# Output products of a fused attention and SwiGLU kernel: 48 plain products a block against seven half products of 2x2 blocks

## The chip, the cores and the metric

The kernel runs on one core of a Trainium2 chip. The metric is the device time of one execution in microseconds. Its engines run side by side, each with a queue of its own, and meet at semaphores: TensorE (PE in the profile, its weight loads PEld), VectorE (DVE), ScalarE (ACT), GpSimd (POOL) and SyncE (SP), which issues DMAs.

## The reference

A linear attention with cosine weights, then an RMS norm and a SwiGLU feed-forward layer. Batch 8, 8 heads, 576 positions, head dimension 64, so 4608 tokens of 512 features; the inner dimension is 1536.

```python
r = maximum(x, 0); phi = concatenate([r * cos_w, r * sin_w], axis=-1)      # for q and k
kv = einsum('bhsf,bhsd->bhfd', k_p, v); z = sum(k_p, axis=2)
attn = einsum('bhsf,bhfd->bhsd', q_p, kv) / (einsum('bhsf,bhf->bhs', q_p, z) + 1e-6)
x = attn as (B * S, H * D)
xn = x / sqrt(mean(x * x) + 1e-6) * rms_g
h = silu(xn @ w_gate) * (xn @ w_val)                                       # 4608 x 1536
out = h @ w_out                                                            # 4608 x 512
```

## The kernel before, in words

The tokens are worked in nine blocks of 512. Blocks 0 to 7 hold 512 positions of one batch each; block 8 holds the tails, the last 64 positions of all eight batches. Before the change the order is 0, 1, 2, 3, 4, 5, 6, 8, 7.

A block has two parts. First come 12 gate and value steps (`gval_step`): step n multiplies the 512 normed tokens with 128 columns of `w_gate` (four matmuls of 512 columns into a psG bank, `half_mm`, L556) and of `w_val` (four into a psV bank). ScalarE takes the silu of the gate (L570), VectorE multiplies it with the value into tile n of `hT` (L571). Then come four output steps (`out_step`): each gives 128 tokens their 512 outputs with 12 matmuls of 512 columns, weights from `hT`, moving operand `wo` (`out_mm`, L574), in psC banks. ScalarE copies the bank to SBUF (L286) and SyncE stores it (L585; 64 rows at a time for blocks 0 and 8, L592). Of block 7, worked last, the last 128 tokens are split by columns into 256, 160 and 96.

The attention of batch b+1 is worked inside block b. The order of all this is written out by hand: `at(blk, n, where, f, ...)` registers a call for a slot of step n of block blk, and `run` makes the calls at that place. "pe" is before the step's matmuls, "mid" between gate and value, "pre" before the silu and the multiply, "post" after them; steps 12 to 15 are the output steps. The order in a slot is the order of registration, and each engine, and SyncE's queue of DMAs, keeps the order in which the calls come.

For one batch the calls are these. The loads of k, v and q for batch nb go to a ring of five `raw` buffers, from SyncE, in steps 0, 3 and 6 of block nb-2 (steps 3, 5, 8 of block 2 and 4, 8, 12 of block 1). `k_phi` makes phi of k (L292 on ScalarE, L294 on VectorE) and `v_cast` rounds v to bf16 (L288), both in the output steps of block nb-2. `q_phi` makes phi of four groups of 128 queries, each followed by a transpose through a DMA of SyncE (`q_tr_dma`, L346): in steps 14, 15, 0 and 1 (for batch 3 one step later). `kvz_pe` makes the key-value products in step 2 (L387, L394). `nd_pe` makes the attention outputs of group j (L449) in steps 4, 6, 8 and 10; `nd_post` divides them on VectorE (L489, L492, L499), `x_sq` sums squares on ScalarE (L515) and takes the power -1/2 on GpSimd (L520), and one step later `x_norm` scales them on VectorE (L527) and `x_tr_dma` transposes them through a DMA (L540) for the next block. The tails of two batches at a time go the same way (`load_q_tails`, `q_tails_phi`, `nd_tails_pe`, L474), spread over blocks 2, 3, 4 and 6.

The program has eight semaphores for DMAs of SyncE, used in turn; a DMA waits for the one issued eight before it.

Of the kernel before, what the change touches and what calls it, by code (L numbers as in the profile page):

```python
# [9 lines left out]
FP32 = mybir.dt.float32  # L10
# [7 lines left out]
def kernel(  # L18
# [15 lines left out]
    P = 128  # L34
# [16 lines left out]
    ring = ctx.enter_context(tc.tile_pool(name="ring", bufs=5))  # L51
    two = ctx.enter_context(tc.tile_pool(name="two", bufs=2))
    four = ctx.enter_context(tc.tile_pool(name="four", bufs=4))
    six = ctx.enter_context(tc.tile_pool(name="six", bufs=6))
# [84 lines left out]
    def load_q_tails(pair):  # L139
        rqt[pair] = two.tile([P, H, D], FP32, name="rqt", tag="rqt")  # L140
# [69 lines left out]
    vv0 = one.tile([P, HP, NC * D], BF16, name="vv0")  # L210
# [61 lines left out]
    vv = one.tile([P, HP, NC, E], BF16, name="vv")  # L272
# [5 lines left out]
    xnT_tail = one.tile([P, NDT, TB], BF16, name="xnT_tail")  # L278
# [73 lines left out]
    def q_tails_tr_dma(pair):  # L352
        t = qp_of(("t", pair))
        qpTt[pair] = one.tile([P, H, P], BF16, name="qpTt", tag="qpTt")
# [82 lines left out]
    def kvz0_evac(eng, g):  # L437
        if 0 not in kvzs:
            kvzs[0] = six.tile([P, 2, HP * E], BF16, name="kvzs", tag="kvzs")
        copy(eng, kvzs[0][:, g, :], psG[g][:, 0 : HP * E])  # L440

    def kvz_evac(eng, b):
        kvzs[b] = six.tile([P, 2, HP * E], BF16, name="kvzs", tag="kvzs")
# [123 lines left out]
    def gval_h(blk, n):  # L567
        g, v = banks_of(blk, n)
        sg = four.tile([P, TB], FP32, name="sg", tag="sg")
# [9 lines left out]
    def out_store(eng, blk, j, bank, cols=(0, DM)):  # L579
        osb = four.tile([P, DM], FP32, name="osb", tag="osb")  # L580
        w = cols[1] - cols[0]
        copy(eng, osb[:, 0:w], bank[:, 0:w])
        if 0 < blk < 8:
            rows = out[blk * S : blk * S + 512, :].rearrange("(p j) m -> p j m", j=4)
            nc.sync.dma_start(out=rows[:, j, cols[0] : cols[1]], in_=osb[:, 0:w])  # L585
            return
        for i in range(2):
            b, c = (0, 2 * j + i) if blk == 0 else (2 * j + i, NC - 1)
            rows = out[b * S + 512 : b * S + S, :]
            if b == 0:  # L590
                rows = out[0:S, :].rearrange("(s c) m -> s c m", c=NC)[:, c, :]
            nc.sync.dma_start(  # L592
                out=rows[:, cols[0] : cols[1]], in_=osb[64 * i : 64 * i + 64, 0:w]
# [70 lines left out]
    def unit_silu(i):  # L664
        sg_of[i] = four.tile([P, TB], FP32, name="sg", tag="sg")
# [95 lines left out]
    KCS5 = ((0, 1), (2,), (3,), (4,))  # L761
# [34 lines left out]
    def last_step():  # L796
# [5 lines left out]
        sg = four.tile([P, TB], FP32, name="sg", tag="sg")  # L802
# [18 lines left out]
    for nb in range(2, B):  # L821
        b = nb - 1
        first = nb == 2
        for i, cs in enumerate(KCS5 if wide(nb) else KCS):
            kb, kn = ((0, 14), (0, 15), (1, 0), (1, 1))[i] if first else (b - 1, 12 + i)
            for c in cs:
                at(kb, kn, "post", k_phi, V, nb, c, 0)
                at(kb, kn, "post", k_phi, A, nb, c, 1)
        for i in range(2):
# [8 lines left out]
        kz = 3 if first else 2  # L838
        at(b, kz, "pe", kvz_pe, nb)
        at(b, kz, "pre", kvz_evac, A, nb)  # L840
        for j in range(4):
            n = ((6, 8, 9, 11) if first else (4, 6, 8, 10))[j]
            at(b, n, "mid" if n == 9 else "pe", nd_pe, nb, j)
            at(b, n, "pre", nd_post, nb, j)
            at(b, n, "post", x_sq, nb, j)
            m = n + 2 if first and j == 0 else n + 1
# [3 lines left out]
    for pair in range(4):  # L850
        b = 2 * pair or 3
        at(*((2, 13), (1, 13), (3, 9), (5, 9))[pair], "post", load_q_tails, pair)
        at(b, 3, "post", q_tails_phi, V, pair, 0)
        at(b, 3, "post", q_tails_phi, A, pair, 1)
        at(b, 3, "post", q_tails_tr_dma, pair)
# [103 lines left out]
```

## Time and profile before

| what | value |
|---|---|
| three runs | 322.76, 323.32 and 323.61 us; median 323.32 |
| profiled execution, span from first to last instruction | 321.1 us |
| what lies around the span, against the median | 2.2 us |
| mean granted TensorE clock | 1.000 |
| blocks 3 and 4 (121.29 to 155.06 and 155.06 to 188.80) | 33.77 and 33.74 us, of which PE is busy 33.56 and 33.53, VectorE 21.57, ScalarE 19.07 |
| HBM read and written | 37.83 and 9.44 MB, 147 GB/s over the span |

The durations below are of that one execution. Busy time of an engine is the time in which it runs instructions; matmuls are pipelined, so the time of many in a row says more than the duration of one (0.38 us each, but 0.86 for four of 512 columns). The chain that ended last is followed back from the last instruction, at each step to what released it. A DMA's landing is the time from its issue to the semaphore that tells of its end; not every DMA has one in the trace.

### The profile page before, as it was taken

To read this page: it belongs to the slowest core of one execution; us is meant where nothing else is said; L and a number is where in the kernel's file an instruction comes from. 1 tells how busy PE (TensorE), PEld (TensorE's weight loads), DVE (VectorE), ACT (ScalarE), POOL (GpSimd) and SP (SyncE) were. 2 spreads that over 40 slices of the span, in tenths; PEclk is the share of its full clock that TensorE was granted. 3 is DMA by queue.
4 is the path that set the end of the run, shared out by engine and by line. 5 is a ranking of instruction groups with operands and counts; after the bars stand their busy time and mean duration, and the time that the engine had idled before them with its cause. 6 is when DMAs were issued, how large, how long until landed. Compare 5 with 4: busy or idle time off the path is not lost.

```text
span 321.1 us, 6023 instructions
## 1 busy us (share of the span) xinstructions
PE 313.6 (98%) x2274; PEld 162.4 (51%) x2310; DVE 185.4 (58%) x382; ACT 165.8 (52%) x322; POOL 40.5 (13%) x79
## 2 busy tenths in 40 slices
PE   7999999999999999999999999999999999999996
PEld 2689564544454445444544445544544444444444
DVE  7976977668457773777457644781676034204410
ACT  5766756754574466554744575446543233223321
POOL 9771211002001100010001100100011000000000
PEclk9999999999999999999999999999999999999999
DMA  7999999788999999999799959995522500041002
GB/s 232 239 270 269 282 329 227 201 183 190 223 226 211 187 263 187 221 247 182 162 186 230 197 163 200 197 217 163 99 59 41 116 33 0 0 102 31 1 35 98
DMA packets 80092, 53.76 MB, mean 167 GB/s; under 512 B 52235, under 2 KB 74047, under 8 KB 80063
## 3 DMA queue, kind: packets, MB, share of 16 engines
q1 hardware_dynamic: 73110, 41.25, 62.1%
q0 software_dynamic: 6944, 12.13, 15.5%
q8 instruction: 18, 0.29, 0.4%
q14 instruction: 12, 0.09, 0.1%
q10 hardware_dynamic: 8, 0.00, 0.0%
HBM read 37.83 MB, written 9.44 MB: 147 GB/s over the span
## 4 chain that ended last, share of the span: by engine, by line
PE 94%; DMA 2%; DVE 1%; issue 1%; POOL 1%; ACT 0%; POOLq 0%; ACTq 0%
PE psC L574 27%; PE psV L556 27%; PE psG L556 26%; PE psV L643 2%; PE psA L449 2%; DMA vv<-in_v_dram 2%; PE psG L574 2%; PE psG L643 2%; PE psA L387 2%; PE psA L394 1%; PE psA L474 0%; PE psV L363 0%; PE psG L430 0%; PE psC L546 0%; POOL raw L135 0%
## 5 line engine op out<-in xcount | busy, mean ns | idle before, releaser
L571 DVE TENSOR_TENSOR hT<-psV,sg 128x512 bf16<-128x512 f32 x99 | 68.2, 689 | 96.5 <-PE psV L556 64.1
L556 PE MATMUL psV<-xnT,wv 128*128 128x512 bf16 x344 | 89.6, 379 | 0.7 <-issue 0.2
L570 ACT ACTIVATE sg<-psG 128x512 f32<-128x512 f32 x99 | 58.6, 592 | 60.8 <-PE psG L556 52.7
L556 PE MATMUL psG<-xnT,wg 128*128 128x512 bf16 x337 | 88.5, 379 | 0.7 <-issue 0.2
L574 PE MATMUL psC<-wo,hT 128*128 128x512 bf16 (+1 forms) x400 | 88.4, 376 | 0.4
L574 PEld LDWEIGHTS <-hT 128*128 128x128 bf16 x456 | 43.1, 98 | 47.7
L556 PEld LDWEIGHTS <-wv 128*128 128x128 bf16 x400 | 39.0, 98 | 46.8
L556 PEld LDWEIGHTS <-wg 128*128 128x128 bf16 x400 | 37.0, 98 | 39.9 <-DVE xnT L288 0.2
L520 POOL TENSOR_TENSOR rs<-ms,mhalf 128x1 f32<-128x1 f32 x36 | 20.5, 570 | 193.9 <-ACT scr L515 193.7
L286 ACT COPY osb<-psC 128x512 f32<-128x512 f32 x32 | 18.7, 585 | 49.9 <-PE psC L574 46.1
L515 ACT ACTIVATE scr<-xt 128x513 bf16<-128x513 f32 x36 | 22.8, 635 | 23.3 <-DVE xt L499 22.3
L527 DVE SCALAR_TENSOR_TENSOR xn<-xt,rs,gb 128x512 bf16<-128x512 f32 (+1 forms) x37 | 26.9, 730 | 9.9 <-POOL rs L520 9.9
L292 ACT ACTIVATE kp<-raw,tab 128x256 bf16<-128x256 f32 (+2 forms) x51 | 28.8, 607 | 2.4 <-DMA raw<-in_k_dram 2.4
L499 DVE TENSOR_TENSOR xt<-psA,rec 128x512 f32<-128x512 f32 x36 | 24.9, 691 | 1.2
L292 ACT ACTIVATE qp<-raw,tab 128x512 bf16<-128x512 f32 (+1 forms) x36 | 23.3, 666 | 1.2 <-DMA raw<-in_q_dram 1.1
L294 DVE TENSOR_SCALAR kp<-raw,tab 128x256 bf16<-128x256 f32 (+2 forms) x53 | 20.1, 428 | 0.5 <-DMA raw<-in_k_dram 0.5
L294 DVE TENSOR_SCALAR qp<-raw,tab 128x512 bf16<-128x512 f32 (+1 forms) x34 | 15.3, 463 | 4.7 <-DMA raw<-in_q_dram 4.7
L449 PEld LDWEIGHTS <-qpT 128*128 128x128 bf16 x224 | 10.6, 97 | 6.6
L556 PE MATMUL psV<-xnT_tail,wv 128*128 128x512 bf16 x48 | 12.3, 379 | 0.1
L556 PE MATMUL psG<-xnT_tail,wg 128*128 128x512 bf16 x46 | 12.0, 379 | 0.1
L288 DVE CAST vv<-raw 116x1280 bf16<-116x1280 f32 (+1 forms) x13 | 11.1, 857 | 1.3 <-DMA raw<-in_v_dram 1.3
L449 PE MATMUL psA<-kvzs,qpT 128*128 128x65 bf16 x224 | 11.4, 193 | 0.0
(102 smaller groups left out, 177.7 us busy)
## 6 DMA issues: line engine op xcount, KB each, us to landing
out_dram<-osb SPq DMA_DIRECT2D x27, 256.0 KB, 2.3
raw<-in_q_dram SPq DMA_DIRECT2D x6, 1024.0 KB, 9.1
raw<-in_k_dram SPq DMA_DIRECT2D x5, 1120.0 KB, 8.8
raw<-in_v_dram SPq DMA_DIRECT2D x5, 1120.0 KB, 9.4
raw<-in_k_dram POOLq DMA_DIRECT2D x2, 1152.0 KB, 19.2
raw<-in_v_dram POOLq DMA_DIRECT2D x2, 1152.0 KB, 15.7
out_dram<-osb SPq DMA_DIRECT2D x17, 128.0 KB, 2.6
wg<-in_moe_w_gate_dram POOLq DMA_DIRECT2D x3, 512.0 KB, 13.8
```

The source lines that it names most:

```text
L286: A.copy(out=o, in_=i)
L292: A.activation(out=out_ap, in_=in_ap, func=AF.Relu, scale=scale)
L294: eng.tensor_scalar(out=out_ap, in0=in_ap, scalar1=scale, scalar2=0.0, op0=ALU.mult, op1=ALU.max)
L449: nc.tensor.matmul(heads[:, g, hp, :], lhsT=qpT[:, h, j * P : (j + 1) * P], rhs=kvzs[b][:, g, hp * E : (hp + 1) * E], start=True, stop=True,)
L499: V.tensor_tensor(out=xt[:, 0:DM].rearrange("p (hp g d) -> p g hp d", g=2, d=D), in0=heads[:, :, :, 0:D], in1=rec[:, :, :].unsqueeze(3).to ...
L515: A.activation(out=scr[:, :], in_=xt[:, 0 : DM + 1], func=AF.Square, scale=1.0 / math.sqrt(DM), accum_out=ms[:, :],)
L520: G.tensor_tensor(out=rs[:, :], in0=ms[:, :], in1=mhalf[:, :], op=ALU.pow)
L527: V.scalar_tensor_tensor(out=xn_of[(b, j)][:, c], in0=x_of[(b, j)][:, c], scalar=rs_of[(b, j)][:, :], in1=gb[:, c], op0=ALU.mult, op1=ALU. ...
L556: nc.tensor.matmul(bank[:, cols[0] : cols[1]], lhsT=w[:, t, n * P : (n + 1) * P], rhs=x[:, t, cols[0] : cols[1]], start=(t == 0), stop=(t ...
L570: A.activation(out=sg[:, :], in_=g[:, 0:TB], func=AF.Silu)
L571: V.tensor_tensor(out=hT[:, n, :], in0=v[:, 0:TB], in1=sg[:, :], op=ALU.mult)
L574: nc.tensor.matmul(bank[:, 0 : cols[1] - cols[0]], lhsT=hT[:, n, j * P : (j + 1) * P], rhs=wo[:, n, cols[0] : cols[1]], start=(n == 0), st ...
```

## The change

The output part of blocks 1 to 8 is made as a product of 2x2 blocks with seven products in place of eight (Strassen's form). Tokens are halved (256 and 256), the inner dimension is halved (`NM` = 6 tiles of 128 each) and the output columns are halved (`HC` = 256). Each of the seven products is made for two groups p of 128 tokens, with 6 matmuls of 256 columns: 84 matmuls a block. The sums of the inputs are tiles of their own: five sums of `wo` (`wsum`, made once, three on GpSimd and two on VectorE) and per block the sums of `hT` halves on VectorE (`s12` in two parts, `s0`, `s3`, `s4`). The sums of the outputs are made in PSUM: products are added onto a bank that ScalarE has copied out in between, or that VectorE or ScalarE has written, and VectorE subtracts at the end (`q_end`).

The rest follows from the room and the time that this takes. `raw` has four buffers, `sg` three, `osb` two of twice the width, `kvzs` eight; `vv`, `vv0` share room with the sums and `xnT_tail`, `qpTt` with `kp5`; the tails' queries are loaded into `raw`. Block 8 is worked last, and all tails are worked in block 7. From batch 3 on, `v_cast` is on GpSimd, `k_phi` is mostly on ScalarE and in slots "act" inside the output part, and `q_phi` with its transposes is in steps 0, 1, 2 and 4, with the attention outputs in steps 3, 5, 7 and 9. The slots of the loads are the same. The core of the diff:

```diff
+    def h_sum12(m0, m1):
+        V.tensor_tensor(
+            out=s12[:, m0:m1, :], in0=hT[:, m0:m1, :], in1=hT[:, NM + m0 : NM + m1, :],
+            op=ALU.add,
+        )
...
+    def prod(i, p, dst, first=False, cols=(0, HC)):
+        c0, c1 = p * P, p * P + HC
+        lhs = {
+            1: (s0, 0, c0), 2: (s12, 0, c1), 3: (hT, 0, c0), 4: (hT, NM, c1),
+            5: (s12, 0, c0), 6: (s3, 0, c0), 7: (s4, 0, c0),
+        }[i]
...
+            nc.tensor.matmul(
+                dst, lhsT=t[:, o + m, c : c + P], rhs=w,
+                start=(first and m == 0), stop=(m == NM - 1), skip_group_check=True,
+            )
...
-            vb, vn = ((0, 15), (1, 0))[i] if first else (b - 1, 13 + 2 * i)
-            at(vb, vn, "post", v_cast, V, nb, (2 * i, 2 * i + 2))
+            for i in range(3):
+                at(b - 1, 12 + 2 * i, "act", k_phi, A, nb, i, 0)
+                at(b - 1, 13 + 2 * i, "act", k_phi, A, nb, i, 1)
+            for i in range(2):
+                at(b - 1, 12, "dve", k_phi, V, nb, 3, i)
+                at(b, 0, "post", k_phi, (V, A)[i], nb, 4, i)
+                vb = (1, 14 + i) if nb == 3 else (b - 1, 8 + 2 * i)
+                at(*vb, "post", v_cast, G, nb, (2 * i, 2 * i + 2))
         for j in range(4):
-            late = j + (nb == 3)
-            qb, qn = (b, 1 + j) if first else (b - (late < 2), (14 + late) % 16)
-            at(qb, qn, "post", q_phi, V, nb, j, 0)
-            at(qb, qn, "post", q_phi, A, nb, j, 1)
-            at(qb, qn, "post", q_tr_dma, nb, j)
+            n = 1 + j if nb == 2 else (0, 1, 2, 4)[j]
+            at(b, n, "post", q_phi, V, nb, j, 0)
+            at(b, n, "post", q_phi, A, nb, j, 1)
+            at(b, n, "post", q_tr_dma, nb, j)
...
-            n = ((6, 8, 9, 11) if first else (4, 6, 8, 10))[j]
+            n = ((6, 8, 9, 11) if nb == 2 else (3, 5, 7, 9))[j]
...
+        at(*((6, 1), (6, 4), (7, 2), (7, 4))[pair], "post", load_q_tails, pair)
+        b, n = 7, 2 * pair + 1
+        at(b, n, "post", q_tails_phi, V, pair, 0)
+        at(b, n, "post", q_tails_phi, A, pair, 1)
+        at(b, n, "post", q_tails_tr_dma, pair)
+        at(b, n + 3, "pe", nd_tails_pe, pair)
...
+        at(b, n + 4, "post", x_norm, 2 * pair + 1, 4)
+        at(b, n + 4, "post", x_tr_dma, 2 * pair + 1, 4)
...
+        if blk and n == NNT - 1:
+            h_sum12(0, NM // 2)
         gval_h(blk, n)
...
+    def out_step(blk):
...
+        def begin(p):
+            bank = bq[p][0]
+            prod(3, p, bank[:, 0:HC], first=True)
+            prod(4, p, bank[:, HC:DM])
+            osb[p] = osb_tile()
+            run(blk, 12 + p, "act")
+            A.copy(out=osb[p][:, mid], in_=bank[:, :])
...
+        h_sum12(NM // 2, NM)
+        begin(0)
+        run(blk, 12, "post")
+        begin(1)
+        q_start(0)
+        h_sum0()
+        run(blk, 13, "post")
+        prod(5, 0, bq[0][0][:, 0:HC])
+        prod(2, 0, bq[0][0][:, HC:DM])
+        run(blk, 14, "act")
+        side(0)
+        q_start(1)
+        h_sum4()
+        prod(5, 1, bq[1][0][:, 0:HC])
+        prod(1, 0, bq[0][1][:, 0:HC])
+        run(blk, 15, "act")
+        A.copy(out=bq[0][1][:, HC:DM], in_=bq[0][1][:, 0:HC])
+        h_sum3()
+        run(blk, 14, "post")
+        prod(2, 1, bq[1][0][:, HC:DM])
+        prod(1, 1, bq[1][1][:, 0:HC])
+        run(blk, 16, "act")
+        side(1)
...
+        run(blk, 12, "dve")
...
+        prod(7, 0, bq[0][1][:, 0:HC])
+        prod(6, 0, bq[0][1][:, HC:DM])
+        q_end(0)
+        prod(7, 1, bq[1][1][:, 0:HC])
+        if blk < last_blk:
+            prod(6, 1, bq[1][1][:, HC:DM])
+            q_end(1)
...
-    for blk in (1, 2, 3, 4, 5, 6, 8, 7):
+    for blk in range(1, 9):
```

`side` copies the two outer sums of a group out of PSUM, `q_start` writes the first two products' sum into the other bank, and in block 8 `side` and `q_end` issue a store for each half of 64 rows and 256 columns: 18 stores in all for that block.

More of the change, by code (lines that the diff above doesn't have):

```diff
@@ L139, in load_q_tails @@
     def load_q_tails(pair):
-        rqt[pair] = two.tile([P, H, D], FP32, name="rqt", tag="rqt")
+        t = ring.tile([P, H * NC5 * D], FP32, name="raw", tag="raw")
+        rqt[pair] = t[:, 0 : H * D].rearrange("p (h d) -> p h d", h=H)
         for i in range(2):
@@ L577, in out_mm, with osb_tile, store @@
         )
[L579 to L582, printed above, removed]
+    def osb_tile():
+        return two.tile([P, 2 * DM], FP32, name="osb", tag="osb")
+    def store(blk, j, cols, src):
         if 0 < blk < 8:
             rows = out[blk * S : blk * S + 512, :].rearrange("(p j) m -> p j m", j=4)
-            nc.sync.dma_start(out=rows[:, j, cols[0] : cols[1]], in_=osb[:, 0:w])
+            nc.sync.dma_start(out=rows[:, j, cols[0] : cols[1]], in_=src)
             return
@@ L591, in out_store @@
                 rows = out[0:S, :].rearrange("(s c) m -> s c m", c=NC)[:, c, :]
-            nc.sync.dma_start(
-                out=rows[:, cols[0] : cols[1]], in_=osb[64 * i : 64 * i + 64, 0:w]
+            nc.sync.dma_start(out=rows[:, cols[0] : cols[1]], in_=src[64 * i : 64 * i + 64])
+    def out_store(eng, blk, j, bank, osb):
+        copy(eng, osb, bank[:, 0:DM])
+        store(blk, j, (0, DM), osb)
+    s12 = hsum[:, 0 : NM * TB].rearrange("p (m s) -> p m s", m=NM)
+    s0, s3, s4 = [
+        hsum[:, NM * (TB + i * HC) : NM * (TB + (i + 1) * HC)].rearrange(
+            "p (m s) -> p m s", m=NM
+        )
+        for i in range(3)
+    ]
@@ L760 @@
     KCS = ((0, 1, 2), (3, 4), (5, 6), (7, 8))
-    KCS5 = ((0, 1), (2,), (3,), (4,))
     for c in range(NC):
@@ L801, in last_step @@
         kvz_pe(1)
-        sg = four.tile([P, TB], FP32, name="sg", tag="sg")
+        sg = three.tile([P, TB], FP32, name="sg", tag="sg")
         A.activation(out=sg[:, :], in_=g[:, 0:TB], func=AF.Silu)
```

177 lines of the change are left out of this document (126 added, 51 removed).

## The prediction

> **What bounds the kernel now.** I read the busy times first, then the chain that ended last, then the chain in order of time, and then the queue of SyncE, because the change moves work past that queue.
>
> ```profile
> PE 313.6 (98%) x2274; PEld 162.4 (51%) x2310; DVE 185.4 (58%) x382; ACT 165.8 (52%) x322; POOL 40.5 (13%) x79
> ...
> PE psC L574 27%; PE psV L556 27%; PE psG L556 26%; PE psV L643 2%; PE psA L449 2%; DMA vv<-in_v_dram 2%; PE psG L574 2%; PE psG L643 2%; PE psA L387 2%; PE psA L394 1%; PE psA L474 0%; PE psV L363 0%; PE psG L430 0%; PE psC L546 0%; POOL raw L135 0%
> ...
> 27.39 1.75 PE psV L643 x16
> ...
> 144.76 5.07 PE psC L574 x23
> 149.88 5.34 PE psC L574 x24
> 155.22 0.86 PE psG L556 x4
> ```
>
> TensorE is busy for 98% and is 94% of the chain. Nothing else ends a wait in the steady state, so a saved matmul is saved time, and any new wait of PE is lost time. The last four lines are the prices. Four 512-column matmuls take 0.86 us, 0.216 each. Sixteen of 256 columns, each with its own weight load, take 1.75, 0.109 each: half price, nothing lost to weight loads.
>
> A block is 12 gate and value steps of 8 matmuls (1.73 us each, 20.75), 1.23 of key-value products, 1.0 of attention outputs and 48 output matmuls (10.37): about 33.4, and 33.8 with a pair of tails.
>
> The queue of SyncE is the other thing to see: its timeline in block 5, landings asked for single issues, and the spread over all query transposes.
>
> ```profile
> 193.87 1.10 SPq L115 DMA_DIRECT2D raw<-in_k_dram  x2
> 195.02 0.80 SPq L119 DMA_DIRECT2D raw<-in_k_dram  x1
> 195.99 1.66 SPq L346 DMA_TRANSPOSE qpT<-qp  x1
> 197.70 4.06 SPq L115 DMA_DIRECT2D raw<-in_v_dram  x2
> ...
> qpT<-qp SPq DMA_TRANSPOSE x1, 7.9
> ...
> raw<-in_k_dram SPq DMA_DIRECT2D x1, 1120.0 KB, 9.2
> ...
> DMA to landing us min/median/max: 3.0/3.2/7.9
> ```
>
> A query transpose lands 3.1 us after its issue. The one at 195.99, issued behind a key load of 1.1 MB, landed after 7.9, 0.8 after the load. Transposes of xn behind loads, issued at 108.48, 138.52 and 169.57, took 8.4, 9.5 and 7.4. So a transpose waits for the load ahead of it in the same queue. Before, only the fourth transpose of a batch stands there, needed at step 10: covered.
>
> VectorE's own pace, from its timeline at the end of block 2:
>
> ```profile
> 110.85 0.69 DVE L571 TENSOR_TENSOR hT<-psV,sg 128x512 bf16<-128x512 f32 x1 [0.76 <-ACT sg L570]
> 111.46 0.74 DVE L527 SCALAR_TENSOR_TENSOR xn<-xt,rs,gb 128x512 bf16<-128x512 f32 x1
> 112.12 0.16 DVE L489 TENSOR_SCALAR rec<-psA 128x8 f32<-128x8 f32 x1
> ```
>
> Instructions overlap a little: a multiply of 0.69 lets the next start after 0.61, an x_norm of 0.74 after 0.66. Queued work is summed with these; what somebody waits for, with the whole duration. A multiply starts 0.27 after its last value matmul (block 7: 307.75 to 308.02), a ScalarE copy 0.2.
>
> **Part by part.** Times are us after a block's start, or after T, the end of its last value matmul.
>
> *Products.* 48 x 0.216 = 10.37 become 84 x 0.109 = 9.12: minus 1.25 in each of 8 blocks, 10.0 in all if PE never waits.
>
> *Sums on VectorE.* Five sums of 128x1536 bf16 a block; no row shows a bf16 tensor_tensor. The f32 one (L571, 512 elements) starts its successor after 0.60, one element a cycle, so 1.67 for 1536. 16-bit copies go at two (L288, 128x1024, 680 ns): 0.87. I take 0.87, the row of the same type. An output step then gives VectorE 5 x 0.87, two starts of 0.34, two ends and the last multiply of 0.60 each, two key phis of 0.40: 7.6 of 9.1 us. It fits; at 1.67 it is 11.6 and doesn't.
> The Trainium skill, "VectorE: DVE Perf Modes", the perf-mode tier table, gives a bf16 tensor_tensor in SBUF two elements a cycle, 1224 ns for 2048, and no faster mode; by it 1536 would be an estimated 957 ns, and the sum would stand.
>
> *Start of the output step.* PE runs in order, and its output products read hT 0 to 11. The last tile was due at the 12th of 512 columns (T+2.4), now at the 12th of 256 (T+1.2). On VectorE, x_norm (0.66) and the first sum (0.87) now stand ahead of its multiply (the multiply before starts at T-1.46: -1.46 + 0.60 + 0.66 + 0.87 = T+0.67, whole at T+1.4): 0.2 lost in blocks 2 to 6. In block 1, with an attention division there too, 1.1. In 7 and 8 nothing.
>
> *Evictions.* ScalarE has six copies (four 585, two about 375) and six key phis (720) a step, 7.0 of 9.1 us; in order each is done 0.5 or more before PE needs its bank. Cost 0; without that cover, PE waits by the amount.
>
> *Query phis in steps 0, 1, 2, 4; products at 3, 5, 7, 9.* The first phi ends at 3.5 (multiply 2.0 to 2.6, key phi, query phi), its transpose lands at 6.6, PE is there at 6.4: 0.2 lost. In blocks 3 to 5 the next key load is issued behind it, after a transpose's 1.25 us of issue, at 4.8. The second transpose, ready at 4.9, comes behind the load's two issues (1.1), at 5.9, and with the 7.95 us of its like at 195.99 lands at 13.85. PE reaches its product at 5 x 1.73 + 1.23 + 0.25 + 0.2 = 10.3: **3.5 lost**. The value load stands ahead of the fourth. Key issue to value landing was 14.5 (98.41 to 112.94) and 15.8 (193.87 to 209.68) with one transpose between; with two, 0.8 more, and 0.84 for the transpose itself, so 4.8 + 16.1 to 17.5 = 20.9 to 22.3. PE comes two products and four steps after the first wait, at 13.85 + 0.5 + 6.92 = 21.3: 0.5 lost. Together 4.2 less 1.05: +3.15 a block, 9.45. In block 6 no such load: -0.85. Bounds: a landing with the quickest key load (8.3 after the load's issue) costs 2.7 and the fourth nothing; 9.5 costs 5.1 and 1.3.
>
> *Value casts on GpSimd.* They wait there for the load, with the pow of the next x_norm (L520) queued behind. Block 2 loads later: keys behind the third transpose (7.8 + 1.25 = 9.1), values landing 14.5 + 0.8 later, 24.4. Then cast 1.27 (1147 ns for 1152 elements), pow 0.57, x_norm 0.66, first sum 0.87, multiply 0.69: hT is whole at 28.5. PE wants it at 20.75 + 1.23 + 1.0 + 0.9 + 1.2 = 25.1: 3.4 lost, and 0.9 at the first and fourth transposes. Block 2: +3.05; from -0.8 (values in time) to +5. In blocks 3 to 5 the cast is over at about 23, before the pow is due.
>
> *Tails in block 7.* The first pair's phi is in step 1 and ends at 4.8, its transpose lands at 7.9, the product is due at 6.9: 1.0 lost. The third pair stands behind x_norm and a transpose's 1.25 us of issue: issued 14.8, landed 17.9, due 15.8: 2.1. Less 1.25: +1.85 (0.3 to 2.9).
>
> *The end.*
>
> ```profile
> L585 SPq DMA_DIRECT2D out_dram<-osb x30: 332/348/531, 80.6 to 318.6; - x30
> ...
> L592 SPq DMA_DIRECT2D out_dram<-osb x16: 466/574/747, 52.1 to 288.4; - x16
> ...
> 318.37 0.26 DVE L288 COPY osb<-psG 128x96 f32<-128x96 f32 x1 [0.86 <-PE psG L574]
> ```
>
> Block 7 was last, with three small stores behind PE: T was 307.75, the span's end T+13.4, 2.5 after the last issue. Now the tails' block is last, and its stores are 64 rows each: 18 issues on SyncE, 0.55 to 0.6 apart back to back (L592 above, against 0.35 for 128 rows). The first follows the fourth product's copy, 36 x 0.109 + 0.2 + 0.585 = T+4.7; 17 steps of 0.56 later the last starts at T+14.2 and the span ends at T+16.7, though VectorE is done at T+9.7: +3.3. At 0.35 apiece +1.1, at 0.58 +3.7.
>
> *At nothing.* Weight sums: nine on GpSimd between 47 us and the first pow of block 1 at 68 (at most 2.4 each by the slowest row per element, L294 POOL); six on VectorE in block 1, 0.6 at most each; if late, x_norm waits 1 or 2 us. Four raw buffers: the tile four back was read a block before. Fifth key phi: done at 3.1, needed at 3.7.
>
> **Sum.** Blocks 1 to 7: -0.15 + 3.05 + 9.45 - 0.85 + 1.85 = +13.35; end +3.3: +16.65 on the profiled 321.1, 337.8. The median of the runs is 2.2 above that span: 340.0. Low bounds together: +4.5, 327.8. High: +27, 350.
>
> **Rivals.**
> *A, PE's count decides (faster).* Nothing on SyncE's queue reaches PE. Place: the landing of the second transpose; it decides from 4.4 us after issue downwards. -0.15, five blocks at -1.05, -1.25, and an end of T+12.2 (-1.2): -7.85, 315.5. For it: the median landing, 3.2. Against: every transpose seen behind a load took 7.4 or more. 0.09.
> *D, transposes pass the loads, the rest stays.* 340.0 less 4.1 in block 2 and 12 in 3 to 5: 323.9, no difference. 0.05.
> *B, sums at one element a cycle.* VectorE's 11.6 sets the output step, 2.3 more in each of eight: 358. For it: the f32 row; against: the 16-bit copies. 0.06.
> *C, the clock falls in PE's new waits.* At the start ten filler matmuls took 3.90 us, where later ten take 2.3; the granted clock reads 1.0 throughout, and PE never idles long again. If each of four waits of about 3.5 us brought such a stretch back, 2 us each: 348. 0.09.
> The Trainium skill, "TensorE: Matmul & The Clock Gate", Part 1, says that about 3.4 us without work returns PE to half clock; nothing here shows it after the start.
> That the products don't shrink is excluded: in the changed program's order each block has 84 output matmuls of 256 columns.
>
> **How the numbers follow.** Forecast, slower by the queue: 0.71. A 0.09 faster; D 0.05 same; all else slower, 0.86. About 0.3%, 1 us, is what can be told from no change. The range, 328 to 350, is the forecast's bounds, with C inside; A, D and B, 0.20, are left out.
>
> **What would show it.** Right: query transposes behind key loads landing near 8 us, PE idle about 3.5 before the second attention product in blocks 3 to 5 and in block 2 before its output step; 18 stores back to back at the end; output steps of 9.3. Wrong: PE idle under 1 us in blocks 3 to 5, then A or D; sums near 1.7 us, B; a granted clock under 1 after the waits, C.

## The result, and the profile after

The changed kernel takes 361.43 us, median of six runs (358.03 to 364.37), against 323.00: a ratio of 1.116, 95% interval 1.112 to 1.121. Forecast were 340.0 and a range of 328 to 350: the sign was right, the size was not. The profiled execution is the longest of the six, 364.37 us with a span of 362.6 and a mean granted clock of 0.967, and the ratio leaves it out.

The lines of the page that answer to those of before (busy times, slices of PE and of its granted clock, chain by engine):

```profile
PE 318.8 (88%) x2580; PEld 191.2 (53%) x2580; DVE 240.1 (66%) x440; ACT 178.3 (49%) x349; POOL 65.5 (18%) x98
...
PEclk9999999999999889899987999899999999999997
...
PE 56%; DMA 15%; DVE 13%; issue 6%; ACT 5%; SPq 1%; POOL 1%; ACTq 0%; DVEq 0%; POOLq 0%
```

PE falls from 94% to 56% of the chain, and the clock row, all nines before, has dips. What PE waited for (total, times, longest):

```profile
PE psA L458 <- DMA qpT<-qp: 13.3, 8, 4.5
PE psG L664 <- DVE hT L580: 9.5, 6, 4.6
PE psA L483 <- DMA kp<-qp: 3.9, 3, 2.0
PE psG L565 <- DVE xnT L296: 2.3, 1, 2.3
```

These are the query transpositions, the start of the output steps, the tails, and block 1's first product. Before, none of them stood in the list, whose longest entry was the first matmul of the program:

```profile
PE psC L598 <- DVE warm L164: 1.2, 1, 1.2
```

By periods (start of a block to the start of the next): the blocks begin 2.7 us later (56.8 against 54.1); block 1 takes 36.5 against 33.4, block 2 41.7 against 33.8, blocks 3 to 5 40.2, 40.0 and 38.8 against 33.8, 33.8 and 33.3, block 6 33.5 against 33.8, and the last two 75.0 together against 65.2. Sum: +41.5 us of span, where the forecast had +16.65.

The second transposition of block 4, in the timeline:

```profile
178.86 1.24 SPq L354 DMA_TRANSPOSE qpT<-qp  x1
...
180.15 1.12 SPq L116 DMA_DIRECT2D raw<-in_k_dram  x2
...
181.44 6.07 SPq L354 DMA_TRANSPOSE qpT<-qp  x2
...
184.91 1.03 PE L565 MATMUL psV<-xnT,wv 128*128 128x512 bf16 x4
...
189.09 0.62 PE L458 MATMUL psA<-kvzs,qpT 128*128 128x65 bf16 x8 [3.15 <-DMA qpT<-qp]
...
189.52 1.90 PE L565 MATMUL psG<-xnT,wg 128*128 128x512 bf16 x4
```

The transposition is issued at 181.44 behind the key load, and its product starts 7.65 later: the wait that was forecast. Measured by the pitch of the matmuls, from the start of the one before the wait to the start of the one after it, it is 3.53 us here, 3.56 in block 5 and 4.89 in block 3; 0.2 of each is the matmul before, so 3.3, 3.3 and 4.7 are lost (forecast 3.5). All waits "by pitch" below are counted like this. But the four matmuls behind it take 1.90, where four of the same shape took 1.03 ahead of it: about half speed. Stretches of the same trace, the columns being busy times by engine, then the granted clock, the DMA share and GB/s:

```profile
123.30:130.10 6.80, 5.94 (x28) 4.10 (x29) 5.39 (x9) 2.80 (x5) 0.00 (x0) 0.50 0.11 22
150.60:154.00 3.40, 3.40 (x11) 1.18 (x8) 1.06 (x3) 1.21 (x3) 0.35 (x1) 0.50 1.11 277
...
188.10:195.00 6.90, 5.92 (x21) 2.38 (x22) 1.75 (x4) 1.34 (x4) 0.55 (x1) 0.51 1.24 241
...
229.10:232.50 3.40, 3.33 (x15) 1.49 (x16) 1.06 (x3) 0.90 (x2) 0.00 (x0) 0.50 1.08 301
```

At each of the four long waits stand 3.4 or 6.8 us at half clock, which begin between 0.9 us before the end of the wait and 0.4 after it: 20.5 us, in which PE is busy for 18.6; half of that is lost, about 9. The six runs point the same way: the quickest had the highest mean clock, 0.982, and the longest one of the lowest, 0.967.

GpSimd's new work is the third thing. The entry to block 1 and the end of block 2:

```profile
50.64 11.25 POOL L624 TENSOR_TENSOR wsum<-wo 128x512 bf16<-128x512 bf16 x9
50.71 1.63 DVE L536 SCALAR_TENSOR_TENSOR xn<-xt,rs,gb 128x512 bf16<-128x512 f32 x1 [0.84 <-POOL rs L529]
...
52.27 3.56 DVE L302 TENSOR_SCALAR kp<-raw,tab 128x256 bf16<-128x256 f32 x3
...
119.13 1.25 POOL L296 CAST vv<-raw 116x1280 bf16<-116x1280 f32 x1 [6.86 <-DMA raw<-in_v_dram]
120.34 0.55 POOL L529 TENSOR_TENSOR rs<-ms,mhalf 128x1 f32<-128x1 f32 x1
...
120.92 1.71 DVE L536 SCALAR_TENSOR_TENSOR xn<-xt,rs,gb 128x512 bf16<-128x512 f32 x1 [3.44 <-POOL rs L529]
...
124.16 0.39 PE L664 MATMUL psG<-wsum,hT 128*128 128x256 bf16 x1 [4.55 <-DVE hT L580]
```

While GpSimd makes the weight sums, an x_norm takes 1.63 (0.74 alone) and three key phis take 3.56. In the timeline of the kernel before those three take 0.87:

```profile
51.10 0.87 DVE L294 TENSOR_SCALAR kp<-raw,tab 128x256 bf16<-128x256 f32 x3
```

The end is one stream of 18 stores issued by SyncE, as forecast; 11.41 by 18 is 0.63 each where 0.56 was taken:

```profile
348.99 11.41 SPq L601 DMA_DIRECT2D out_dram<-osb  x18
```

### The profile page after: what moved, and what is told of

Its sections match the earlier page's. It is cut to its first block, busy times and chain, and to the rows that moved or that the text cites. A ratio compares the mean times of both kernels' runs of the same rounds, so it can differ in the third digit from the quotient of the medians.

```text
span 362.6 us, 6739 instructions
## 1 busy us (share of the span) xinstructions
PE 318.8 (88%) x2580; PEld 191.2 (53%) x2580; DVE 240.1 (66%) x440; ACT 178.3 (49%) x349; POOL 65.5 (18%) x98
## 4 chain that ended last, share of the span: by engine, by line
PE 56%; DMA 15%; DVE 13%; issue 6%; ACT 5%; SPq 1%; POOL 1%; ACTq 0%; DVEq 0%; POOLq 0%
PE psG L565 14%; PE psV L565 12%; PE psC L664 10%; DMA qpT<-qp 7%; PE psG L664 4%; PE psV L664 4%; DVE xn L536 4%; DMA raw<-in_v_dram 2%; DVE xt L508 2%; ACT scr L524 2%; DMA hsum<-in_v_dram 2%; PE psV L716 2%; DMA kp<-qp 2%; PE psG L716 2%; DVE hT L580 2%
## 5 line engine op out<-in xcount | busy, mean ns | idle before, releaser
L565 PE MATMUL psG<-xnT,wg 128*128 128x512 bf16 x352 | 93.9, 390 | 3.4 <-DVE xnT L296 2.3
L664 PEld LDWEIGHTS <-hsum 128*128 128x128 bf16 x486 | 47.8, 99 | 6.5 <-DVE hsum L641 0.2
L300 ACT ACTIVATE kp<-raw,tab 128x256 bf16<-128x256 f32 (+2 forms) x61 | 36.5, 626 | 2.4 <-DMA raw<-in_k_dram 2.4
L536 DVE SCALAR_TENSOR_TENSOR xn<-xt,rs,gb 128x512 bf16<-128x512 f32 (+1 forms) x37 | 31.8, 862 | 5.2 <-POOL rs L529 5.2
L664 PEld LDWEIGHTS <-hT 128*128 128x128 bf16 x192 | 18.9, 101 | 15.5 <-DVE hT L580 11.2
L302 DVE TENSOR_SCALAR kp<-raw,tab 128x256 bf16<-128x256 f32 (+1 forms) x43 | 21.2, 540 | 0.5 <-DMA raw<-in_k_dram 0.5
L664 PE MATMUL psG<-wsum,hT 128*128 128x256 bf16 x96 | 12.9, 274 | 9.5 <-DVE hT L580 9.5
L664 PE MATMUL psV<-wsum,hsum 128*128 128x256 bf16 (+1 forms) x150 | 18.8, 270 | 0.0
L664 PE MATMUL psC<-wsum,hsum 128*128 128x256 bf16 x138 | 17.7, 273 | 0.0
L1010 DVE TENSOR_TENSOR osb<-psV,osb 128x512 f32<-128x512 f32 x8 | 5.5, 690 | 15.8 <-ACT kp L300 8.4
```

What stands on the lines that cost most here:

```text
L300: A.activation(out=out_ap, in_=in_ap, func=AF.Relu, scale=scale)
L302: eng.tensor_scalar(out=out_ap, in0=in_ap, scalar1=scale, scalar2=0.0, op0=ALU.mult, op1=ALU.max)
L536: V.scalar_tensor_tensor(out=xn_of[(b, j)][:, c], in0=x_of[(b, j)][:, c], scalar=rs_of[(b, j)][:, :], in1=gb[:, c], op0=ALU.mult, op1=ALU. ...
L565: nc.tensor.matmul(bank[:, cols[0] : cols[1]], lhsT=w[:, t, n * P : (n + 1) * P], rhs=x[:, t, cols[0] : cols[1]], start=(t == 0), stop=(t ...
L664: nc.tensor.matmul(dst, lhsT=t[:, o + m, c : c + P], rhs=w, start=(first and m == 0), stop=(m == NM - 1), skip_group_check=True,)
```

## The experiments

Sixteen kernels were run. Names in the diffs are those of the quoted code.

**Keys one block earlier.** Is the key load ahead of the transposition what PE waits for?

```diff
+            if which == "k" and nb > 4:
+                at(b - 1, 12, "post", load_kv, which, nb)
+                continue
```


> The changed kernel with one move: the key loads that stood behind the first query transpose in blocks 3, 4 and 5 are issued in the output part of the block before (blocks 2, 3, 4), everything else the same. Theory (a query transpose waits on the DMA queue for the key load ahead of it): PE's waits at the second attention product, 4.9, 3.5 and 3.6 us in blocks 3 to 5, go, and with them the stretches of half clock behind them (3.4, 6.8 and 3.4 us, half of each lost, 6.8); up to 0.7 us a block may come back at the fourth transpose, behind the value load. 361.4 becomes 343 to 346. Rival (the transposes are late because the phis are made late, whatever stands ahead of them): less than 3 us gained, the waits stay over 2.5 us each.

346.99 us, ratio 1.074 (1.072 to 1.077). Blocks 3 to 5 fall to 34.4, 34.4 and 34.5 us. Block 4, in one stretch, at full clock:

```profile
167.60:202.00 34.40, 32.34 (x251) 19.59 (x253) 24.88 (x44) 19.84 (x38) 4.61 (x6) 1.00 0.75 177
```

The three long waits had cost 11.3 us and the half clock at them some 6; the periods fell by 15.7, because 1.7 came back in the shorter waits, most of it at the start of the output steps. The mechanism is as expected, the total 1 us above the forecast of 343 to 346. The run doesn't tell whether the order of the queue or the transfers themselves held the transposition up: moving the load takes both away.

**Fillers in the wait.** Fifteen matmuls whose results nobody reads, ahead of the late product, so that PE isn't idle there.

```diff
+            if j == 1 and nb > 3:
+                at(b, n, "pe", filler, 15, psC[1])
```


> The changed kernel, with 15 filler matmuls of 512 columns (3.2 us at full clock) into an idle PSUM bank just before the second attention product of blocks 3 to 6, where PE waits 4.9, 3.5, 3.6 and under 0.3 us. Theory (the half clock behind these waits comes from PE standing idle): the granted clock stays 1.0 in blocks 3 to 5, 6.8 us come back there, and block 6, which has no such wait, pays about 3: 357 to 358.5, with PE's idle stretch before the product under 1.8 us each. Rival (the slow stretches come from something else, such as the load on the whole chip): the clock falls all the same and the time rises by about 3, 364.

365.91 us, ratio 1.132. Stretches of blocks 3, 4 and 5:

```profile
133.80:172.50 38.70, 35.65 (x266) 21.01 (x268) 25.07 (x44) 19.89 (x38) 4.61 (x6) 1.00 0.74 157
172.50:211.10 38.60, 35.65 (x266) 21.02 (x268) 25.07 (x44) 19.89 (x38) 4.61 (x6) 1.00 0.74 158
211.10:251.70 40.60, 37.13 (x266) 21.50 (x268) 25.16 (x44) 19.77 (x38) 4.61 (x6) 0.96 0.66 150
```

In blocks 3 and 4 the clock stays at 1.00 and the periods are 1.5 shorter: with PE kept at work the clock does not fall. (In the five kernels that have these two waits without fillers, half clock came at block 3's in all and at block 4's in three.) In blocks 5 and 6 the first transposition came late too, waits of 2.47 and 1.98 by pitch ahead of any filler, and in block 5 the clock fell there. So the total, which lies near the rival's 364, says nothing for either theory. Why that first transposition was later is open.

**Weight sums all on VectorE.**

```diff
...
-                   w_sum, G, i, m, m + 2)
...
+            at(1, (i * 3 + m // 2) * 10 // 14, "post", w_sum, V, i, m, m + 2)
```


> The changed kernel with all fifteen sums of the output weights on VectorE, spread over steps 0 to 10 of block 1, none on GpSimd. Theory (GpSimd's nine sums of 1.28 us slow VectorE's instructions while both run, 50.6 to 61.9 us: three key phis took 3.56 us against 0.87 before): VectorE's key phis and value casts go back to their durations of before, and block 1 ends about 4 us earlier, 357. Rival (VectorE is slow there for what it does itself): the phis stay slow, and nine more sums at 0.33 each cost up to 3 us, 361 to 364.

357.65 us, ratio 1.109 (1.104 to 1.114): 3.8 less. Block 1 starts at 53.9 (56.8 before this edit) and its gate steps fall from 25.0 to 23.4; its output step grows from 11.6 to 12.5, because VectorE now makes nine sums of 0.42 us more in block 1. At the entry to block 1 the x_norm takes 0.75 again and the three key phis 0.87:

```profile
50.23 0.75 DVE L536 SCALAR_TENSOR_TENSOR xn<-xt,rs,gb 128x512 bf16<-128x512 f32 x1 [0.84 <-POOL rs L529]
50.89 0.87 DVE L302 TENSOR_SCALAR kp<-raw,tab 128x256 bf16<-128x256 f32 x3
```

GpSimd's weight sums did hold VectorE up.

**Only the late phis, in the kernel before.** Plain products, sums and casts as they were; q_phi in steps 0, 1, 2, 4 and attention products in 3, 5, 7, 9.

```diff
-            qb, qn = (b, 1 + j) if first else (b - (late < 2), (14 + late) % 16)
+            qb, qn = (b, 1 + j) if first else (b, (0, 1, 2, 4)[j])
-            n = ((6, 8, 9, 11) if first else (4, 6, 8, 10))[j]
+            n = ((6, 8, 9, 11) if first else (3, 5, 7, 9))[j]
```


> The kernel before with one part of the change alone: from batch 3 on the query phis and their transposes in steps 0, 1, 2 and 4 of the block that uses them, the attention outputs in steps 3, 5, 7 and 9; products, sums, casts, tails and order of blocks as before. Theory (the moved transposes behind the key load are what costs most): waits of PE of 3.5 to 5 us at the second attention product of blocks 3 to 5, half clock behind them, and 0.6 at the first: 323 becomes 338 to 343. Rival (the output sums and the casts are what makes the transposes late, not their place): under 327.

344.79 us, ratio 1.067 (1.065 to 1.069), a little above the forecast's 338 to 343. So a loss of more than half the size, 21.7 of 38.4 us, comes without any Strassen. The waits are there, and half clock at three of them, though not all where they were expected: the longest are 3.65 by pitch in block 2 and 3.78 in block 3, then 2.53 in block 4 and 2.24 in block 5 (the kernel's list of waits, and one stretch):

```profile
PE psA L449 <- DMA qpT<-qp: 15.2, 8, 3.4
```
```profile
110.80:114.20 3.40, 2.88 (x14) 1.33 (x15) 1.51 (x4) 0.72 (x2) 0.18 (x1) 0.50 1.12 278
```

**Tails spread, sums behind hT, two queues at the end.** Three single edits of the changed kernel:

```diff
-        at(*((6, 1), (6, 4), (7, 2), (7, 4))[pair], "post", load_q_tails, pair)
-        b, n = 7, 2 * pair + 1
+        at(*((6, 1), (6, 4), (6, 7), (6, 10))[pair], "post", load_q_tails, pair)
+        b, n = 7, 2 * pair
```


> The changed kernel with one edit: the tails' query loads and phi products spread over more steps, so that each phi stands further behind its load. In the changed kernel PE waits 1.39, 2.38 and 1.25 us in the block that carries the tails (its gate step is 26.7 us where a gate step without waits is about 22 us), beside the weight sums that VectorE then has to do anyway. Theory (the tails' phi stands too close behind its loads and their transposes): the gate step falls to about 22.5 us, and the total by about 4.2 us, to about 357. Rival (the transposes land late wherever the loads are put, because the queue is what is late): under 1 us gained, total 360.5 to 362.

356.24 us, ratio 1.101 (1.097 to 1.106). Block 7 takes 31.8, where it took 35.9, and no longer waits for the tails. As expected.

```diff
-        if blk and n == NNT - 1:
-            h_sum12(0, NM // 2)
...
+        h_sum12(0, NM // 2)
         h_sum12(NM // 2, NM)
```


> The changed kernel with one edit: the first half of the sums of hT is made at the start of the output step, and no longer ahead of the last hT multiply, so the last multiply no longer stands behind those sums on VectorE. In the changed kernel PE waits at the start of the output steps 1.17 us in block 1, 1.43 to 1.44 in blocks 3 to 5, 0.86 in block 6, and the last part of a wait of 4.82 in block 2. Theory (the sums ahead of the last hT multiply are what makes the first product late): most of these go, about 6 us in all, total about 355.5. Rival (the first products that need the sums then wait instead, at product five): under 2 us gained, total above 359.

356.79 us, ratio 1.104 (1.103 to 1.106). In blocks 3 to 5 the waits at the start of the output steps fall from 1.43 to 0.57 by pitch, and the steps from 10.5 to 9.6. As expected, in the order and nearly in the size.

```diff
+            eng = nc.scalar if blk == 8 and i else nc.sync
```


> The changed kernel with one edit: in the last block the stores of the second half of the rows are issued from ScalarE's queue, the others from SyncE's as before. In the changed kernel 18 stores of 64 rows each follow one another at 0.637 us on one queue, from T+4.7 to T+15.6 (T the end of the last product), while VectorE has its last result ready at T+9.7. Theory (the issue of one queue sets the end): the end comes at about T+14 and no longer at T+18.4, total about 357. Rival (the transfers themselves or the last results set it): under 1.5 us gained, total above 359.5.

356.38 us, ratio 1.101 (1.097 to 1.105). The end comes at T+14.7 in place of T+18.4 (T is the end of the block's last value matmul): the issue of one queue did set it.

**All of it together**, with block 2's loads and attention products moved as well (loads at steps 4, 6 and 9 of block 1, products at 4, 6, 8 and 10).

> The changed kernel with six edits together: the keys' loads one block earlier, batch 2's attention products spread with their loads earlier, the tails spread, the first sums of hT at the start of the output step, all sums of the weights on VectorE, and the last block's stores on two queues. It computes the same as the changed kernel. Theory (the seven half products do save PE's time, about 1.25 us a block, and everything above that was waits that the moved steps bring, and the half clock that follows the long ones): blocks 2 to 7 have periods of 32.5 to 33.5 us, no stretch at half clock, total 316 to 325, so about the kernel before. Rival (the added work on VectorE is itself the limit, and the waits come back at other places): periods of 35 us or more in blocks 2 to 5, total above 335.

328.31 us, ratio 1.016 (1.014 to 1.017): between the two bands, nearer to the theory's. The long waits are gone and the page's clock row is all nines again. But blocks 2 to 5 take 33.6 each, the 33.3 to 33.8 of the kernel before, and block 1 takes 37.5. So about 33 of the 38 us were waits, the half clock at them, GpSimd's work beside VectorE and the end; and in blocks 2 to 5 the products still save nothing.

**One late key load put back**, batch 6's, in that kernel.

```diff
-            if which == "k" and nb > 3:
+            if which == "k" and nb > 3 and nb != 6:
```


> The six edits of the run before, less one load: the keys of batch 6 are loaded at step 0 of block 4, as in the changed kernel, so that only there a transposition stands behind a load. Theory (a wait of PE of 3.5 to 4.9 us costs itself and then half of the stretch of half clock that follows, 1.7 or 3.4 us): block 4 grows from 33.6 to 38.5 to 40 us, with one stretch of 3.4 or 6.8 us at half clock and none elsewhere. Rival (the clock falls for another reason, such as the added work on the other engines): block 4 grows by the wait alone, 3.5 to 4 us, at full clock.

333.39 us against 328.31. Blocks 3 and 4, and a stretch within block 4:

```profile
125.20:158.80 33.60, 32.61 (x254) 19.50 (x253) 24.56 (x44) 19.87 (x38) 4.60 (x6) 1.00 0.64 146
158.80:196.70 37.90, 34.38 (x255) 20.00 (x254) 24.81 (x44) 19.87 (x38) 4.60 (x6) 0.95 0.83 192
173.50:176.90 3.40, 3.40 (x10) 1.21 (x8) 1.27 (x2) 1.21 (x3) 0.55 (x1) 0.51 1.09 293
```

One load moved, one wait of 3.4 us (by pitch), one stretch of 3.4 us at half clock, 4.3 us in the block: a little below the band, because 0.6 us of shorter waits in that block went away with it. The mechanism of the main loss is shown by itself.

**Where do the saved matmuls go?** Three kernels: plain products at both ends and later attention products (`out_plain` is the output part of the kernel before); the later attention products alone; and plain products everywhere, on the schedule of the first. The diff is the first one's, against the kernel with six edits.

```diff
-            n = ((4, 6, 8, 10) if nb == 2 else (3, 5, 7, 9))[j]
+            n = (4, 6, 8, 10)[j]
...
-        out_step(blk)
+        (out_plain if blk in (1, last_blk) else out_step)(blk)
...
-            at(1, (i * 3 + m // 2) * 10 // 14, "post", w_sum, V, i, m, m + 2)
+            at(1 + t // 8, 1 + t % 8, "post", w_sum, V, i, m, m + 2)
```


> The six edits of the run before, and three more: block 1 and the last block make their output by the plain eight half products' worth of full products, so the sums of the weights are needed only in block 2 and are spread on VectorE over the gate steps of blocks 1 and 2; and the attention products stand at steps 4, 6, 8 and 10 in every block. Theory (with its waits gone the change saves PE about 1 us in each of the blocks 2 to 7; the edges cost more than they saved): block 1 falls from 37.5 to about 33.5 us, the last block's end from 14.7 us to about 13.5 after the gate step, and the first attention product's wait of 0.75 us goes in blocks 2 to 6; span about 318, total about 320, so some 1% below the kernel before. Rival (the sums on VectorE cost in the gate steps what the products save): blocks 2 to 6 stay at 33.6 us, total 322 to 326.

> The six edits of the run before and one more: the attention products stand at steps 4, 6, 8 and 10 in every block, and no longer at 3, 5, 7 and 9 in blocks 2 to 6. In the run before PE waits 0.74 to 0.83 us for the first of them in each of those blocks, 3.4 us behind the issue of its transposition. Theory (a step more covers it): these waits go, 0.7 us by 5, total about 324.8. Rival (the later x_norm comes nearer to the last hT multiplies, and the wait moves to the start of the output step): under 1 us gained, total above 327.

> The same as the kernel with plain edges, but with the plain output products in all blocks: the schedule of the loads, phi products and attention products is the same, and no seven half products are left anywhere (the sums of the weights are still made, unused). It measures what the seven half products are worth by themselves. Theory (PE bound at 10.4 us against 9.2 us of an output step): blocks 2 to 7 about 1 us longer each than in the kernel with plain edges, total 6 us above it, near 325 to 326. Rival (VectorE and ScalarE bound the output steps, so the sums take back what the products save): within 1.5 us of the kernel with plain edges.

327.0 us (ratio 1.010 to 1.014), 329.05 (1.017 to 1.021) and 325.92 (1.007 to 1.013). The rivals held, the first a little above its band; there the last block's end stayed near T+14.7, as its stores are still 64 rows each. Moved by themselves, the later attention products take the waits out of the gate steps (23.8 to 22.9 us in block 4) and bring them back in the output steps (9.7 to 10.8). On this schedule plain products everywhere are as good as seven half products. The timeline of the kernel with plain ends, at the end of block 4's gate steps, says why:

```profile
181.23 1.25 POOL L296 CAST vv<-raw 116x1280 bf16<-116x1280 f32 x1
181.77 1.25 DVE L536 SCALAR_TENSOR_TENSOR xn<-xt,rs,gb 128x512 bf16<-128x512 f32 x1
...
182.95 1.81 DVE L631 TENSOR_TENSOR hsum<-hT 128x1536 bf16<-128x1536 bf16 x2
...
183.95 0.50 PE L665 MATMUL psG<-wo,hsum 128*128 128x256 bf16 x3 [0.45 <-DVE hsum L631]
...
184.82 1.16 PE L665 MATMUL psG<-wo,hsum 128*128 128x256 bf16 x9 [0.37 <-DVE hsum L631]
```

The sums of hT stand behind an x_norm that nobody needs before the next block, and that takes 1.25 in place of 0.74 while a cast runs on GpSimd; the next kernels test both.

**VectorE's queue relieved**: three kernels more, against the kernel with plain ends. The casts on ScalarE, and from batch 4 on one step earlier (the diff's first part); the last x_norm behind the first sums (the two parts after it); and both, with the weight sums in block 1's output step (all four parts).

```diff
-                vb = (1, 14 + i) if nb == 3 else (b - 1, 8 + 2 * i)
-                at(*vb, "post", v_cast, G, nb, (2 * i, 2 * i + 2))
+                vb = (1, 14 + i) if nb == 3 else (b - 1, 7 + 2 * i)
+                at(*vb, "post", v_cast, A, nb, (2 * i, 2 * i + 2))
...
-            m = n + 1
+            m = 13 if j == 3 else n + 1
             at(b, m, "post", x_norm, nb, j)
...
-                at(b - 1, 13 if nb == 4 else 12, "post", load_kv, which, nb)
+                at(b - 1, 14, "post", load_kv, which, nb)
...
-            at(1 + t // 8, 1 + t % 8, "post", w_sum, V, i, m, m + 2)
+            at(1, 12 + t // 4, "post", w_sum, V, i, m, m + 2)
```


> The kernel with plain edges, with one edit: the values' casts go from GpSimd to ScalarE. In the kernel with plain edges the last x_norm, right ahead of the sums, takes 1.25 us in blocks 2 to 5, where a cast of 1.25 us runs on GpSimd beside it, and 0.74 us in block 6, where there is none. Theory (GpSimd's work beside it doubles x_norm, and the sums are late by that): x_norm is 0.74 us everywhere, the output steps fall from 10.8 to about 10.0 us, total about 3 us less, 324. Rival (the casts do not matter, or ScalarE's own queue then makes hT late): under 1 us.

> The kernel with plain edges, with one edit: the last x_norm of each block (with its transposition, and the keys' loads behind it) goes behind the first sums of the output step; the casts stay on GpSimd. Theory (the order of VectorE's queue makes the sums late): the waits of 0.72 and 0.64 us for the sums shrink to under 0.3 each and the output steps fall from 10.8 to 9.6 us, total 321 to 323. Rival (the transposition, issued later, lands too late for the next block's first products): a new wait of 1 us or more at the start of blocks 3 to 6, total not below 326.

> The kernel with plain edges, and three edits more: the values' casts go from GpSimd to ScalarE, the last x_norm of a block (with its transposition, and the keys' loads behind it) goes behind the first sums of the output step, and the weight sums go to VectorE in block 1's output step, where it has little else. In the kernel with plain edges the output steps of blocks 2 to 5 take 10.8 us, with waits of 0.57, 0.72 and 0.64 us for hT and its sums, and the last x_norm takes 1.25 us beside a cast and 0.74 without one. Theory (those waits are VectorE's queue ahead of the sums, not its total): the output steps fall to 9.2 to 9.6 us, periods of blocks 3 to 5 from 33.7 to about 32.3, block 2 from 35.1 to about 33, total 319 to 321.5. Rival (VectorE's or ScalarE's total is the bound): periods stay above 33.3, total above 324.

The casts alone: 324.72 us, 2.3 less. The x_norms in the kernel with plain ends, and then with the casts moved (durations in ns: least, median, most):

```profile
L536 DVE SCALAR_TENSOR_TENSOR xn<-xt,rs,gb x37: 480/742/1252, 16.3 to 281.1; 128x512 bf16<-128x512 f32 x35, 128x256 bf16<-128x256 f32 x2
```
```profile
L536 DVE SCALAR_TENSOR_TENSOR xn<-xt,rs,gb x37: 477/743/752, 16.4 to 278.7; 128x512 bf16<-128x512 f32 x35, 128x256 bf16<-128x256 f32 x2
```

The order alone: 324.88, 2.1 less and above its band of 321 to 323; one wait for the sums goes and one of 0.64 stays. Together **321.44 us, ratio 0.994 (0.992 to 0.996)**: 0.6% below the kernel before. Its timeline at the same place:

```profile
176.96 0.69 DVE L580 TENSOR_TENSOR hT<-psV,sg 128x512 bf16<-128x512 f32 x1 [0.76 <-ACT sg L579]
177.57 1.82 DVE L631 TENSOR_TENSOR hsum<-hT 128x1536 bf16<-128x1536 bf16 x2
...
179.17 1.47 PE L665 MATMUL psG<-wo,hsum 128*128 128x256 bf16 x12
...
180.51 0.75 DVE L536 SCALAR_TENSOR_TENSOR xn<-xt,rs,gb 128x512 bf16<-128x512 f32 x1
```

No wait ahead of PE's twelve, and the output steps of blocks 4 to 6 take 9.2 us.

**What the products are worth there.** The same kernel with `out_plain(blk)` in every block.

> The same as the kernel with plain edges and VectorE relieved, but with the plain output products in all blocks (the sums of the weights are still made, unused). Its pair has periods of 32.1 to 33.3 us in blocks 2 to 7 with output steps of 9.2 to 10.0 us, and took 321.44. Theory (with the sums no longer late, the seven half products save most of PE's 1.25 us in each of six blocks): output steps of 10.4 us, blocks 2 to 7 near 33.3 us, total 326 to 328. Rival (the moved steps bring the gain, whatever the products): within 1.5 us of 321.4.

329.93 us, ratio 1.022 (1.019 to 1.024): 8.5 more, and above the band. That is not all the products' worth. Its pair is the kernel of 321.44 us. In the profiled runs the spans differ by 9.8, and 4.2 of that is an accident in block 4 (37.5 us, clock 0.95): PE waited 2.7 by pitch for a transposition that was issued 5 us behind a key load, with its product 7.0 behind the issue; its pair has no such wait there. What stays is 5.6 in six blocks, from output steps of 10.4 against 9.2 to 10.0. The run of 329.93 itself had a clock of 1.000, so what it lost beyond the products is open. Block 6 of this kernel and of its pair:

```profile
227.00:260.30 33.30, 33.09 (x213) 16.29 (x216) 16.50 (x33) 15.95 (x31) 2.19 (x4) 1.00 0.50 112
```
```profile
219.00:251.10 32.10, 32.10 (x254) 19.71 (x252) 22.90 (x42) 16.19 (x32) 2.19 (x4) 1.00 0.49 116
```

That is 1.2 us in this block: PE's 1.25, at last. In the others it is less, down to nothing in block 5, where the pair waits 1.4 by pitch for an attention product.

## Why the prediction was wrong

*Products and sums* were right in length. Undisturbed output steps take 9.2 us (forecast 9.12), a sum 0.95 (0.87 taken). Rival B is out. That a saved matmul is saved time held only once VectorE's queue was relieved: until then the sums came late and took the saving back. The estimate from the Trainium skill, "VectorE: DVE Perf Modes", the perf-mode tier table, was 0.957, and the trace agrees.

*The transpositions behind key loads* were right and are the main cause: 3.5 forecast; 4.7, 3.3 and 3.3 lost; undone by moving the load. For the fourth transposition, 0.5 forecast, PE never waited in blocks 3 to 5; for the first it lost 0.4 and not 0.2.

*Rival C is the step that failed most.* I gave the clock 0.09 because nothing in the trace of before had idled long enough to show it, and held it beside the forecast as another case. It is no case of its own: it came with the very waits that the forecast contained, and should have been priced on each of them. The sum priced each wait with its own length and put nothing for the clock; it took about 9 us. The Trainium skill, "TensorE: Matmul & The Clock Gate", Part 1, had said so: idle PE returns to half rate. The stretches of 3.4 and 6.8 us agree with its window of about 3.4; shorter waits could suffice here (below).

*"At nothing: weight sums"* failed. I priced GpSimd's time and not what it does to VectorE beside it: about 2.7 us were lost at the entry and 3 in block 1. Moving them to VectorE gave back 3.8. The rest fits the sums' own time on VectorE, but no run separates it: with six edits, and no sums on GpSimd, block 1 still took 37.5 us, and with plain products there, and the sums spread over blocks 1 and 2, 34.1. The Trainium skill, "SBUF — State Buffer", section "SBUF: two separate sides", says that GpSimd and a VectorE instruction with two SBUF inputs lock the same ports for a whole instruction. The trace agrees in the main: the x_norm at 181.77, 0.74 long alone, ended 0.54 after the cast ended at 182.48, and the hT products, which read PSUM, kept their 0.69.

*The start of the output step*, forecast at 0.2, lost 1.3 in blocks 3 to 5, and 4.7 in block 2 (forecast 3.4). The chain was drawn rightly, cast, power, x_norm, sum, multiply, but x_norm was 1.25 to 1.71 in place of 0.66, again with a cast on GpSimd beside it.

*Tails*: 1.0 and 2.1 forecast; 1.2, 2.2 and a third of 1.0 lost. *End*: +3.3 forecast, +5.0 measured: 0.63 an issue in place of 0.56 makes 1.3 of the difference.

Together, the profiled run lies 24.8 us above the forecast's sum: about 9 are half clock, 5.9 the entry and block 1, 5 the start of the output steps, 1.7 the end, 1.3 the tails, and the rest smaller waits. The range took in the bounds of the waits and not their consequences, and so ended at 350.

## What to carry to other kernels

A change that saves the engine that sets the time 3% of its work may add no more than that in waits, so follow each moved step through the queues it enters, and price every long wait of TensorE with the half clock that can come with it. Two idle engines are not two free engines: work for GpSimd is priced by the VectorE instructions that run beside it. When a gain is missing, look at what stands ahead of the needed instruction in its queue and put there only what is needed soon.

## What the runs showed of the hardware

The clock could fall at waits much shorter than the 3.4 us of a stretch. Over all kept traces, behind block 0 and by pitch, none of eight waits from 1.98 to 2.40 us brought half clock, nine of 16 from 2.41 to 3.42 did, and all 19 from 3.44 up did. In between, the same wait at the same place may or may not bring it: a wait of 2.66, at block 1's first product, was followed by half clock in the kernel with fillers and not in the changed kernel:

```profile
57.00:60.40 3.40, 3.39 (x9) 1.15 (x9) 3.40 (x4) 1.39 (x3) 3.40 (x4) 0.51 0.86 188
```
```profile
57.00:60.40 3.40, 3.40 (x17) 1.57 (x16) 3.40 (x4) 2.18 (x5) 3.40 (x4) 1.00 0.79 175
```

A wait of 3.42 in block 4 of the kernel with the tails spread passed at full clock, where the 3.41 of the kernel with one late key load did not. What decides is open. It may be why runs of one kernel differ by 6 us, but no trace of a second run was kept to show it. The Trainium skill, "TensorE: Matmul & The Clock Gate", Part 1, names one idle window of about 3.4 us as the condition; by these runs less can be enough, and the waits that were always safe here stayed at 2.40 or less by pitch, 2.2 without the matmul before. The half clock can begin a microsecond after PE has resumed: in the kernel with one late key load PE works again at 172.5, and the stretch is 173.5 to 176.9.
